# A sparse-attention and expert-router kernel: K turned a step later, rank products a step part earlier, x's first turnings around q's, and V gathered from joined rows

## The chip, the cores and the metric

The kernel runs on one core of one Trainium2 chip. The metric is device time in microseconds (us) of one launch; a profiled execution gives the trace. Engines: PE (TensorE matmul, PEld its weight loads), DVE (VectorE), ACT (ScalarE), POOL (GpSimd), SP (SyncE, whose queue issues nearly all DMAs). L with a number is a line of the kernel before.

## The reference, cut

```python
# 4 batch items, 8 heads, 768 rows, head size 64, blocks of 32 rows
scores = scale * q @ k.T                       # per batch item and head
# kept: own block and its neighbours, first and last block of rows and of keys, 3 sampled blocks per row block
attn = softmax(where(mask, scores, -1e9)) @ v
x = attn.transpose(0, 2, 1, 3).reshape(3072, 512)
# router: 8 experts, cosine similarity, argmax, softmax weight of the chosen one
for e in range(8):
    rows = expert_idx == e
    out[rows] = gate[rows, None] * (maximum(x[rows] @ w1[e], 0) @ w2[e])   # w1 512x1024, w2 1024x512
```

## The kernel before, in words

**Work units.** Attention works in 24 chunks of 128 query rows of one batch item. Two chunks of the same rows from two batch items form a pair (`pair_chunk`, 12 pairs; pairs 0 to 5 are batch items 0 and 1, pairs 6 to 11 items 2 and 3). `attention_fast` runs one loop of steps s; step s scores chunk `TURNS[s]` (order 0, 2, 1, 3, 4, 5, ...), weighs the chunk scored a step before, and turns x of the one before that. So pair p is scored in steps 2p and 2p+1 and weighed in 2p+1 and 2p+2 (p of 2 and more).

**A step on PE, in the program's order** (every engine runs its own queue in this order): `score_near` (tile `ac`, L580, L583), `score_far` (`dps`, L605, needs `kg`, gathered K columns), `turn_x` (`xg_ps`, L740), `turn_q` of the next chunk (the bank `yp`, L544; DVE evicts it in two copies, L549), `turn_k` for the K groups of table `turning` (`kps`, L526 for the first half, L532 for the second), `planned(0)`, `weigh_far` (`av<-vg,pd`, L660: the first use of a pair's gathered V), the rest of the weighing, `normalize` on DVE, `planned(1)`. In the steps that follow a chunk with the first and last blocks, `score_ends` (`bps`) comes in too.

**What sets the order.** `planned` runs entries (step, part, function) that `after_step` writes for the routing of a pair: among them `rank` (L891, L893), two small products into the same bank `yp` that turned q uses, once for each of the first three groups of six chunks; its three DVE operations read that bank. `fill_slots` (L980) uses the bank too. POOL writes `seen` (L864), which `rank` reads.

**V.** `vt[m]` holds six tiles of V of the present two batch items, 128 rows x 2 x 8 x 65 floats (64 values and a column of ones); `load_v` fills them by table `values_at` for the second half. `gather_v` brings, for each block of a pair and each of its 3 samples, 32 rows of V from DRAM into `vg_ring`, two buffers: twelve DMAs a pair (six where the pair has the first and last blocks), each of 32 x 16 runs of 64 floats. SP issues them in `fetch_all` (L497 for other loads between them, L499 for the gathers), six in step 2p-2 and the rest in step 2p-1, each behind the release of the buffer that pair p-2 used. Pair 2's twelve are all issued in step 3. `x_dram<-x` (L881) is on SP as well and waits for DVE.

The experts' stage follows from about 250 us: 23 tiles of 128 rows, two large products each.

```python
def gather_v(k, s, i=None):
    a, c = pair_chunk(s)
    t, src = k.vg_ring[s % 2], of_seq(k.v, a, i)
    for r in range(NRAND):
        for g, shift in zip(blocks_of(c), shifts(k, mybir.EngineType.SP, r, c)):
            yield in_pair(t[lanes_of(r, g), g], i)[:, :, 0:D], src[bass.ds(shift, BLK)]
```

Of the kernel before, what the change touches and what calls it, by code (L numbers as in the profile page):

```python
# [12 lines left out]
F32 = mybir.dt.float32  # L13
# [8 lines left out]
B, H, S, D = 4, 8, 768, 64  # L22
BLK = 32
NB = S // BLK
NRAND = 3
NC = S // P
# [24 lines left out]
VW = H * (D + 1)  # L51
NI = NB - 2
NCH = B * NC
DUO = 2
NS = NCH // DUO
TURNS = [0, 2, 1, 3, *range(4, NCH)]
DEN_LOW, DEN_HIGH = 0.1, 1e10
NEG = -1.0e9
LGAT = 80
# [323 lines left out]
def lanes_of(slot, g):  # L383

    if slot < 2:
        return slice(BLK + slot, NRAND * BLK, 2)
    return slice(0, BLK) if (slot + g) % 2 == 0 else slice(NRAND * BLK, P)
# [35 lines left out]
def in_pair(t, i=None):  # L423

    return t.rearrange("p i h e -> p (i h) e") if i is None else t[:, i]
# [58 lines left out]
def gather_v(k, s, i=None):  # L484

    a, c = pair_chunk(s)
    t, src = k.vg_ring[s % 2], of_seq(k.v, a, i)
    for r in range(NRAND):
        for g, shift in zip(blocks_of(c), shifts(k, mybir.EngineType.SP, r, c)):
            yield in_pair(t[lanes_of(r, g), g], i)[:, :, 0:D], src[bass.ds(shift, BLK)]  # L490


def fetch_all(k, gathers, loads):

    for i, (to, src) in enumerate(gathers):
        if i % 2 == 0 and loads:
            k.nc.sync.dma_start(out=loads[0][0], in_=loads[0][1])  # L497
            loads = loads[1:]
        k.nc.sync.dma_start(out=to, in_=src)  # L499
    for to, src in loads:  # L500
        k.nc.sync.dma_start(out=to, in_=src)
# [37 lines left out]
def turn_q(k, n):  # L539

    raw = in_pair(k.raw["q", n // DUO], n % DUO)
    ps = bank(k, "q_ps").rearrange("p (j t) -> p j t", t=P)
    for j in range(NPAIR):
        k.nc.tensor.transpose(ps[:, j], raw[:, 2 * j:2 * j + 2, :].rearrange("p h d -> p (h d)"), k.ident)  # L544
    k.qt[n] = t = k.qt_ring[k.queries % 2]
    k.queries += 1
    for h in range(2):
        rows = slice(D * h, D * (h + 1))
        k.nc.vector.tensor_copy(out=t[rows, :, h], in_=ps[rows])  # L549
# [185 lines left out]
def turn_x(k, n):  # L735

    s, i = divmod(n, DUO)
    ps = ring(k, "xg_ps", 0, 1, k.eps, [P, ND, P])
    for j in range(ND):
        k.nc.tensor.transpose(ps[:, j], k.x[s][:, i, j, 0:P], k.ident)  # L740
    if i == 0:
        k.xt[s] = k.xt_pool.tile([P, ND, DUO, P], F32, name="xt", tag="xt", bufs=1)
    k.nc.vector.tensor_copy(out=k.xt[s][:, :, i], in_=ps)  # L743
# [543 lines left out]
def after_step(n, b):  # L1287

    s = TURNS.index(DUO * b + 1) + 2
    steps = route(n, b)  # L1290
    routing = partial(next, steps, None)
    plan = [(s, 1, routing), (s + 1, 1, routing), (s + 2, 0, routing), (s + 2, 0, routing), (s + 2, 1, routing)]
    if s + 3 < NCH:
        plan += [(s + 3, 0, routing)]
    else:
        n.unwritten.append(steps)
    if b % (NC // DUO) == NC // DUO - 1 and b < NS - 1:
        plan += [(s + 3, 0, partial(rank, n, b // (NC // DUO)))]
    if DUO * (b + 1) == EARLY * NC:
        n.dispatching = partial(next, dispatch_early(n), None)  # L1300
        plan += [(s + 3 + (i + 1) // 3, int((i + 1) % 3 > 0), n.dispatching) for i in range(18)]
        plan += [(s + 9, 0, partial(fetch_rows, n, 0))]
        n.first_weights = fetch_weights(n, 0, 0, 4)
        plan += [(s + 7 + i, 1, partial(next, n.first_weights)) for i in range(4)]
        plan += [(s + 10, 1, partial(prepare, n, 0))]
    return [(min(when, NCH), part if when <= NCH else 1, what) for when, part, what in plan]


def attention_fast(n, ctx):
# [64 lines left out]
    nc.gpsimd.memset(zero, 0.0)  # L1374
    nc.sync.dma_start(n.x_dram[N:N + 1, :], zero)

    turning = {0: (4, 5), 1: (6, 7), 10: (8, 9), 11: (10, 11, 12), 12: (13, 14, 15)}
    keys_at = {2: (8, 9), 3: (10,), 4: (11,), 5: (12,), 6: (13,), 10: (14, 15)}
    values_at = {7: (0,), 8: (1,), 9: (2,), 11: (3,), 13: (4,), 15: (5,)}
    routed = {TURNS.index(DUO * b + 1) + 2: b for b in range(NS - 1)}  # L1380
    plan = []
    for s in range(NCH + 1):
        now, after, last, past = (TURNS[i] if 0 <= i < NCH else None for i in (s, s + 1, s - 1, s - 2))
        if s in routed:
            plan = after_step(n, routed[s]) + [p for p in plan if p[0] >= s]
# [6 lines left out]
        def keys_gathered():  # L1392
            if after is not None:
                gather_k(n, after)

        ends = last is not None and place(last)[1] == 0
        late_keys = s in turning and s > 0
        if now is not None:
            score_near(n, now)
            score_far(n, now)  # L1400
# [5 lines left out]
        if past is not None and past >= 2 * DUO:  # L1406
            turn_x(n, past)
        elif past is not None and past % DUO:
            turn_x(n, past - 1)
            turn_x(n, past)  # L1410
        if ends:
            score_ends(n, last, 0)
            score_ends(n, last, 2)
        elif after is not None:
            turn_q(n, after)
        for g in turning.get(s, ()):
            turn_k(n, g)
        if late_keys:
            keys_gathered()
        planned(0)  # L1420
        if s == 0:
            stack_ends(n, 1, (0, 1), 0)
# [23 lines left out]
        if ends:  # L1446
            weigh_ends(n, last, (0, 2))
            score_ends(n, last, 1)
            score_ends(n, last, 3)
            if after is not None:  # L1450
                turn_q(n, after)
        ahead, odd = s // DUO + 1, s % DUO
        loads, gathers = [], ()
        if s in (2, 3):
# [18 lines left out]
        for m in values_at.get(s, ()):  # L1473
            loads += load_v(n, 1, m)
        fetch_all(n, gathers, loads)
        if ends:
            weigh_ends(n, last, (1, 3))
        if last is not None:
# [173 lines left out]
@with_exitstack  # L1652
def kernel(
    ctx: ExitStack,
    tc: tile.TileContext,
    q: bass.AP,
    k: bass.AP,
    v: bass.AP,
    sampled_blocks: bass.AP,
    moe_expert_emb: bass.AP,  # L1660
    moe_tau: bass.AP,
    moe_w1: bass.AP,
    moe_w2: bass.AP,
    out: bass.AP,
):
    assert tuple(q.shape) == (B, H, S, D) and tuple(out.shape) == (N, DM)
    assert tuple(moe_w1.shape) == (E, DM, F) and tuple(sampled_blocks.shape) == (NB, NRAND)
    n = Net()
    n.tc, n.nc = tc, tc.nc
    n.q, n.k, n.v, n.blocks, n.out = q, k, v, sampled_blocks, out  # L1670
    n.emb, n.tau, n.w1, n.w2 = moe_expert_emb, moe_tau, moe_w1, moe_w2
    n.loaded, n.vs, n.es, n.ets, n.sums, n.x, n.rows, n.weights = {}, {}, {}, {}, {}, {}, {}, {}

    n.raw, n.nsq, n.lg, n.turned_rows, n.relu = {}, {}, {}, {}, None
    n.kt, n.qt, n.kg, n.pac, n.pd, n.pb, n.av, n.xt = ({} for _ in range(8))
    n.exact = n.attending = False
    n.const = ctx.enter_context(tc.tile_pool(name="const", bufs=1))
    n.x_dram = tc.dram_tile([N + 1, XW], F32, name="x_dram")
    n.dens = n.const.tile([P, NCH, H], F32, name="dens")

    fast(n)
    todo = n.nc.values_load(n.todo[0:1, 0:1], min_val=0, max_val=2)
    with tc.If(todo > 0):
        more(n)
# [32 lines left out]
```

## Time and profile before

| what | value |
| --- | --- |
| median of 3 runs | 625.15 us (624.96 to 627.76) |
| the profiled execution | 619.32 us, span 617.6 us |
| mean granted TensorE clock | 0.992 of full |
| busy | PE 583.4, DVE 244.6, POOL 244.6, ACT 146.4 us |
| DMA | 170.6 MB in 177,073 packets, 135,432 of them under 512 B |
| steps' starts | 0: 14.7, 1: 28.4, 2: 45.6, 3: 50.2, 4: 64.7, 5: 73.3, 7: 89.7, 9: 105.9, 13: 144.3, 15: 161.0, 17: 179.0, 22: 218.4 us |

The page says how long each engine was busy and cuts the span into 40 slices of 15.4 us. The view of waits lists what each engine stood still for, the timeline shows the instructions of an engine in order with the idle time ahead of them in brackets, and the view of windows gives busy time, granted clock and DMA load of chosen stretches. A step's start is the first `ac` product of its chunk.

### The profile page before, as it was taken

How to read it: one execution, taken by the hardware profiler on the slowest of the kernel's cores; microseconds unless marked ns; L12 is line 12 of the kernel's file. 1: busy time of each engine (PE TensorE's matmuls, PEld its weight loads, DVE VectorE, ACT ScalarE, POOL GpSimd, SP SyncE). 2: the span in 40 equal slices, each digit the busy share in tenths (PEclk: the TensorE clock that was granted, in tenths of full speed). 3: DMA queues.
4: the chain of work that ended last, by engine and by line, in shares of the span. 5: the costliest groups of instructions: out<-in, count | busy, mean ns of one | idle time of the engine just before them, and what ended most of it. 6: DMA issues, size and time to landing. Idle time of an engine off the chain costs nothing.

```text
span 617.6 us, 18763 instructions
## 1 busy us (share of the span) xinstructions
PE 583.4 (94%) x7732; PEld 451.8 (73%) x7732; DVE 244.6 (40%) x743; ACT 146.4 (24%) x287; POOL 244.6 (40%) x474
## 2 busy tenths in 40 slices
PE   7699999998989988999999999999999999999995
PEld 5588888887888977777766777755777636777772
DVE  4424667577879962457211121112122121121110
ACT  2346555565645544100000000000000000000000
POOL 2728347446766330320333334443333333334432
PEclk9799999999999999999999999999999999999999
DMA  9998798999999851899999999998999998999611
GB/s 201 235 171 192 150 169 179 187 198 210 199 196 203 180 193 39 266 402 393 406 400 392 408 396 324 340 327 307 404 408 390 398 381 309 395 400 408 226 36 35
DMA packets 177073, 170.60 MB, mean 276 GB/s; under 512 B 135432, under 2 KB 137608, under 8 KB 174162
## 3 DMA queue, kind: packets, MB, share of 16 engines
q1 hardware_dynamic: 170706, 155.61, 81.2%
q0 software_dynamic: 5216, 13.43, 6.0%
q8 instruction: 63, 1.03, 0.7%
q10 hardware_dynamic: 1056, 0.26, 0.2%
q14 instruction: 32, 0.26, 0.1%
HBM read 156.65 MB, written 12.90 MB: 275 GB/s over the span
## 4 chain that ended last, share of the span: by engine, by line
PE 75%; DVE 9%; DMA 5%; SPq 4%; ACT 2%; issue 2%; POOL 1%; POOLq 0%; DVEq 0%; ACTq 0%
PE hp L1218 26%; PE yp L1231 25%; PE av L660 7%; PE dps L605 4%; SPq L499 3%; PE hp L1263 2%; PE yp L1283 2%; DVE qt L549 2%; PE ac L580 2%; DMA vg<-in_v_dram 2%; DMA w<-in_moe_w_dram 2%; PE ac L583 2%; PE kps L526 1%; PE xg_ps L740 1%; DVE xt L743 1%
## 5 line engine op out<-in xcount | busy, mean ns | idle before, releaser
L1218 PEld LDWEIGHTS hp<-xgt,w 128*128 128x128 f32 x1472 | 167.8, 192 | 10.9 <-issue 10.2
L1218 PE MATMUL hp<-xgt,w 128*128 128x128 f32 x1472 | 169.2, 275 | 0.3 <-DMA w<-in_moe_w_dram 0.3
L1231 PE MATMUL yp<-w,h 128*128 128x512 f32 x368 | 162.0, 592 | 0.0
L1231 PEld LDWEIGHTS yp<-w,h 128*128 128x128 f32 x368 | 68.1, 190 | 76.6 <-issue 76.3
L1142 POOL DMA_INDIRECT xg<-x_dram,quarter x88 | 89.2, 1014 | 32.3 <-issue 27.4
L1244 POOL DMA_INDIRECT out_dram<-y,slot_l x20 | 20.5, 1023 | 156.0 <-DVE y L1243 156.0
L1221 ACT ACTIVATE h<-hp 128x512 f32<-128x512 f32 x23 | 13.7, 597 | 283.1 <-PE hp L1218 280.2
L1225 DVE TENSOR_SCALAR h<-hp 128x512 f32<-128x512 f32 x23 | 15.9, 691 | 126.8 <-PE hp L1218 126.8
L562 POOL COPY kg<-kt 128x128 f32 x176 | 43.8, 299 | 33.5 <-ACT kt L528 23.1
L1243 DVE TENSOR_SCALAR y<-yp,gate 128x512 f32<-128x512 f32 x20 | 15.0, 751 | 102.2 <-PE yp L1231 90.1
L511 POOL COPY vg<-vt 32x1040 f32<-32x1040 f32 (+1 forms) x45 | 43.1, 958 | 21.4 <-PE av L660 14.5
L605 PEld LDWEIGHTS dps<-qt,kg 128*64 128x64 f32 x1408 | 46.7, 138 | 0.0
L605 PE MATMUL dps<-qt,kg 128*64 128x64 f32 x1408 | 45.8, 222 | 0.0
L583 PE MATMUL ac<-qt,kt 128*64 128x256 f32 (+1 forms) x192 | 42.4, 364 | 1.2 <-ACT kt L536 1.2
L580 PE MATMUL ac<-qt,kt 128*64 128x128 f32 x352 | 42.8, 273 | 0.3 <-DVE qt L549 0.3
L580 PEld LDWEIGHTS ac<-qt,kt 128*64 128x64 f32 x352 | 37.9, 137 | 0.6 <-issue 0.5
L549 DVE COPY qt<-yp 64x512 f32<-64x512 f32 x48 | 32.8, 683 | 12.1 <-PE yp L544 11.7
L610 ACT ACTIVATE pd<-dps,bias 128x256 f32<-128x256 f32 x88 | 34.7, 476 | 8.5 <-PE dps L605 8.3
L660 PE MATMUL av<-vg,pd 128*32 128x65 f32 x1408 | 27.5, 221 | 4.1 <-DMA vg<-in_v_dram 2.0
L660 PEld LDWEIGHTS av<-vg,pd 128*32 128x32 f32 x1408 | 22.3, 109 | 8.8 <-issue 4.4
L660 PEld LDWEIGHTS av<-st,pac 128*64 128x64 f32 x704 | 22.8, 137 | 5.8 <-issue 4.8
L730 ACT ACTIVATE pac<-x 128x512 f32<-128x512 f32 x24 | 15.1, 631 | 49.5 <-DVE x L725 49.5
(244 smaller groups left out, 629.4 us busy)
## 6 DMA issues: line engine op xcount, KB each, us to landing
w<-in_moe_w_dram SPq DMA_DIRECT2D x52, 2048.0 KB, 15.2
vg<-in_v_dram SPq DMA_DIRECT2D x132, 128.0 KB, 4.4
kraw<-in_k_dram SPq DMA_DIRECT2D x32, 192.0 KB, 4.6
x_dram<-x SPq DMA_DIRECT2D x10, 516.0 KB, 5.2
qraw<-in_q_dram SPq DMA_DIRECT2D x9, 512.0 KB, 6.2
w<-in_moe_w_dram SPq DMA_DIRECT2D x8, 512.0 KB, 5.1
vt<-in_v_dram SPq DMA_DIRECT2D x10, 256.0 KB, 5.7
vt<-in_v_dram SPq DMA_DIRECT2D x5, 512.0 KB, 6.6
```

The source lines that it names most:

```text
L511: k.nc.gpsimd.tensor_copy(out=k.vg_ring[s % 2][lanes_of(NRAND, g), g, which(i)], in_=k.vt[m][rows, which(i)])
L549: k.nc.vector.tensor_copy(out=t[rows, :, h], in_=ps[rows])
L562: copy(out=t[:, :, g, lanes_of(s, g)], in_=kt[:, :, bass.ds(shift, BLK)])
L580: nc.tensor.matmul(out[0:D, j, half], lhsT=kt[:, j, at:at + D], rhs=qt[:, j, :, D * half:D * (half + 1)], start=True, stop=True)
L583: nc.tensor.matmul(out[D:P, j, half:2].rearrange("p f h t -> p h f t"), lhsT=kt[:, j, S:S + D], rhs=qt[:, j, :, D * half:P].rearrange("p h ...
L605: nc.tensor.matmul(out[D * r:D * (r + 1), NG * j + g], lhsT=kg[:, j, g, D * r:D * (r + 1)], rhs=qt[:, j, :, cols], start=True, stop=True)
L610: nc.scalar.activation(e[:, :, g].rearrange("p j h t -> p j (h t)"), out.rearrange("p (j g) h t -> p j g (h t)", g=NG)[:, :, g], ACT.Exp, ...
L660: k.nc.tensor.matmul(av[lanes, h // NPAIR, h % NPAIR * P:h % NPAIR * P + D + 1], lhsT=lhsT, rhs=rhs, start=first[0], stop=last, skip_group ...
L1142: k.nc.gpsimd.indirect_dma_start(out=x[:, g], out_offset=None, in_=quarters, in_offset=bass.IndirectOffsetOnAxis(ap=k.quarter[:, g, t:t + ...
L1218: nc.tensor.matmul(hp[:, f, :], lhsT=w1[:, d, (f0 + f) * P:(f0 + f + 1) * P], rhs=xt[:, d, :], start=(d == 0), stop=(d == ND - 1))
L1231: nc.tensor.matmul(yp, lhsT=h[:, f, :], rhs=w2[:, f, :], start=(f == 0), stop=(f == NF - 1))
L1244: k.scattered = nc.gpsimd.indirect_dma_start(out=k.out[:, :], out_offset=bass.IndirectOffsetOnAxis(ap=slot, axis=0), in_=y[:, :], in_offse ...
```

## The change

Four things, by tables and by the order of calls:

- **K's turning**: groups 4 to 7 (batch item 1) were turned two in step 0 and two in step 1; now all four in step 1, and in the steps with end blocks behind the last `score_ends` and `turn_q` (`turn_keys`).
- **x's first turnings**: in steps 4 and 5 two chunks of x are turned; the second now comes behind `turn_q`.
- **Rank products**: from `planned(0)` of step s + 3 to `planned(1)` of step s + 2, so to the end of the step before.
- **V in joined rows**: `join_v` writes the six tiles `vt` to a DRAM tensor `joined[a]` of 768 rows x 1040 floats (4160 bytes), for the first half behind the gathers of step 3, for the second in steps 12 (three tiles) and 13 (three). The gathers of pairs 3, 4, 5, 8, 9, 10 and 11 read whole rows of it, 32 per DMA. V's tiles of the second half are loaded sooner: two in step 8, one in each of steps 9, 10 and 11.

```diff
--- before.py
+++ after.py
@@ -54,6 +54,7 @@
 DUO = 2
 NS = NCH // DUO
 TURNS = [0, 2, 1, 3, *range(4, NCH)]
+JOINED = (3, 4, 5, 8, 9, 10, 11)
 DEN_LOW, DEN_HIGH = 0.1, 1e10
 NEG = -1.0e9
 LGAT = 80
@@ -487,7 +488,16 @@
     t, src = k.vg_ring[s % 2], of_seq(k.v, a, i)
     for r in range(NRAND):
         for g, shift in zip(blocks_of(c), shifts(k, mybir.EngineType.SP, r, c)):
-            yield in_pair(t[lanes_of(r, g), g], i)[:, :, 0:D], src[bass.ds(shift, BLK)]
+            if s in JOINED:
+                yield t[lanes_of(r, g), g].rearrange("p i h e -> p (i h e)"), k.joined[a][bass.ds(shift, BLK)]
+            else:
+                yield in_pair(t[lanes_of(r, g), g], i)[:, :, 0:D], src[bass.ds(shift, BLK)]
+
+
+def join_v(k, a, m):
+
+    rows_of = k.vt[m].rearrange("p i h e -> p (i h e)")
+    return [(k.joined[a][lo:lo + rows.stop - rows.start], rows_of[rows]) for rows, lo in pieces(m)]
 
 
 def fetch_all(k, gathers, loads):
@@ -1295,7 +1305,7 @@
     else:
         n.unwritten.append(steps)
     if b % (NC // DUO) == NC // DUO - 1 and b < NS - 1:
-        plan += [(s + 3, 0, partial(rank, n, b // (NC // DUO)))]
+        plan += [(s + 2, 1, partial(rank, n, b // (NC // DUO)))]
     if DUO * (b + 1) == EARLY * NC:
         n.dispatching = partial(next, dispatch_early(n), None)
         plan += [(s + 3 + (i + 1) // 3, int((i + 1) % 3 > 0), n.dispatching) for i in range(18)]
@@ -1374,9 +1384,10 @@
     nc.gpsimd.memset(zero, 0.0)
     nc.sync.dma_start(n.x_dram[N:N + 1, :], zero)
 
-    turning = {0: (4, 5), 1: (6, 7), 10: (8, 9), 11: (10, 11, 12), 12: (13, 14, 15)}
+    turning = {1: (4, 5, 6, 7), 10: (8, 9), 11: (10, 11, 12), 12: (13, 14, 15)}
     keys_at = {2: (8, 9), 3: (10,), 4: (11,), 5: (12,), 6: (13,), 10: (14, 15)}
-    values_at = {7: (0,), 8: (1,), 9: (2,), 11: (3,), 13: (4,), 15: (5,)}
+    values_at = {7: (0,), 8: (1, 2), 9: (3,), 10: (4,), 11: (5,)}
+    joined_at = {3: (0, range(NC)), 12: (1, range(3)), 13: (1, range(3, NC))}
     routed = {TURNS.index(DUO * b + 1) + 2: b for b in range(NS - 1)}
     plan = []
     for s in range(NCH + 1):
@@ -1394,7 +1405,14 @@
                 gather_k(n, after)
 
         ends = last is not None and place(last)[1] == 0
-        late_keys = s in turning and s > 0
+        late_keys = s in turning
+
+        def turn_keys():
+            for g in turning.get(s, ()):
+                turn_k(n, g)
+            if late_keys:
+                keys_gathered()
+
         if now is not None:
             score_near(n, now)
             score_far(n, now)
@@ -1407,16 +1425,15 @@
             turn_x(n, past)
         elif past is not None and past % DUO:
             turn_x(n, past - 1)
-            turn_x(n, past)
         if ends:
             score_ends(n, last, 0)
             score_ends(n, last, 2)
         elif after is not None:
             turn_q(n, after)
-        for g in turning.get(s, ()):
-            turn_k(n, g)
-        if late_keys:
-            keys_gathered()
+        if past is not None and past < 2 * DUO and past % DUO:
+            turn_x(n, past)
+        if not ends:
+            turn_keys()
         planned(0)
         if s == 0:
             stack_ends(n, 1, (0, 1), 0)
@@ -1449,6 +1466,7 @@
             score_ends(n, last, 3)
             if after is not None:
                 turn_q(n, after)
+            turn_keys()
         ahead, odd = s // DUO + 1, s % DUO
         loads, gathers = [], ()
         if s in (2, 3):
@@ -1473,6 +1491,9 @@
         for m in values_at.get(s, ()):
             loads += load_v(n, 1, m)
         fetch_all(n, gathers, loads)
+        if s in joined_at:
+            a, some = joined_at[s]
+            fetch_all(n, (), [piece for m in some for piece in join_v(n, a, m)])
         if ends:
             weigh_ends(n, last, (1, 3))
         if last is not None:
@@ -1676,6 +1697,7 @@
     n.exact = n.attending = False
     n.const = ctx.enter_context(tc.tile_pool(name="const", bufs=1))
     n.x_dram = tc.dram_tile([N + 1, XW], F32, name="x_dram")
+    n.joined = [tc.dram_tile([S, DUO * VW], F32, name=f"joined{a}") for a in range(B // DUO)]
     n.dens = n.const.tile([P, NCH, H], F32, name="dens")
 
     fast(n)
```

**PE, the end of step 0 and the start of step 1.** `kps` is K being turned, `ac` and `dps` are scores. Before:

```order
L605 MATMUL dps<-qt_117,kg 64x64 x16
L544 MATMUL yp_245<-ident,qraw 128x128 x4
L526 MATMUL kps<-ident,kraw 64x128 x24
L580 MATMUL ac<-qt_118,kt_103 64x128
L583 MATMUL ac<-qt_118,kt_103 64x2x2x64
```

And of the change, the same place and then the later one in step 1:

```order
L615 MATMUL dps<-qt_119,kg 64x64 x16
L554 MATMUL yp_247<-ident,qraw 128x128 x4
L590 MATMUL ac<-qt_120,kt_105 64x128
L593 MATMUL ac<-qt_120,kt_105 64x2x2x64
L590 MATMUL ac<-qt_120,kt_105 64x128 x2
...
L637 MATMUL bps<-qt_119,kt_105 64x128 x2
L637 MATMUL bps<-qt_119,kt_105 128x128 x5
L646 MATMUL bps<-qt_119,kt_105 64x64 x24
L554 MATMUL yp_247<-ident,qraw 128x128 x4
L536 MATMUL kps<-ident,kraw 64x128 x48
L670 MATMUL av<-vt_106,pb_113 64x65
```

Step 1's scores now follow q's turning at once; K's four groups (x48) stand between the second turning of q and the second half of the ends' weighing.

**SP, the end of step 3 and the start of step 4.** Before, the last gathers of pair 2 (`vg_113`) and the first of pair 3 (`vg_114`):

```order
L499 DMA vg_113<-in_v_dram 32x16x64
L499 ISA
L499 DMA vg_113<-in_v_dram 32x16x64
L395 TENSOR_LOAD offset
L497 DMA kraw<-in_k_dram 128x6x64
L499 ISA
L499 DMA vg_114<-in_v_dram 32x16x64
```

Of the change:

```order
L509 DMA vg_115<-in_v_dram 32x16x64
L511 DMA joined_61<-vt_106 32x1040
L511 DMA joined_61<-vt_106 96x1040
L511 DMA joined_61<-vt_107 128x1040
L511 DMA joined_61<-vt_108 128x1040
L511 DMA joined_61<-vt_109 128x1040
L511 DMA joined_61<-vt_110 128x1040
L511 DMA joined_61<-vt_111 128x1040
L396 TENSOR_LOAD offset
L507 DMA kraw<-in_k_dram 128x6x64
L509 ISA
L509 DMA vg_116<-joined_61 32x1040
```

Seven writes come in between, and the first gather of pair 3 reads what they write.

**PE, the rank products of the third group.** Before, in step 22 behind q's turning, while the slot products (`lanes`, 12 of them) end step 21:

```order
L772 MATMUL av<-sel,part 128x8 x2
L740 MATMUL xg_ps_1330<-ident,x 128x128 x4
L544 MATMUL yp_245<-ident,qraw 128x128 x4
L891 LDWEIGHTS ones_b
L891 MATMUL yp_245<-seen,ones_b 128x56
L893 LDWEIGHTS before
L893 MATMUL yp_245<-oh,before 128x48
L660 MATMUL av<-vg_113,pd 32x65 x32
```

Of the change, at the end of step 21, ahead of the slot products:

```order
L670 MATMUL av<-st_117,pac 64x65 x16
L901 LDWEIGHTS ones_b
L901 MATMUL yp_247<-seen,ones_b 128x56
L903 LDWEIGHTS before
L903 MATMUL yp_247<-oh,before 128x48
L990 LDWEIGHTS lanes
L990 MATMUL yp_247<-val,lanes 128x10
```

Rank and slot products use the same bank `yp`, now one right behind the other.

## Rows read from the trace of the kernel before

**Rows 1.** The page, busy time of each engine and DMA slices (15.4 us each).

```profile
PE 583.4 (94%) x7732; PEld 451.8 (73%) x7732; DVE 244.6 (40%) x743; ACT 146.4 (24%) x287; POOL 244.6 (40%) x474
...
DMA  9998798999999851899999999998999998999611
```

**Rows 2.** Waits of PE over the span: us in total, times, longest us.

```profile
PE kps L526 <- DMA kraw<-in_k_dram: 5.2, 1, 5.2
PE yp L891 <- DVE qt L549: 4.0, 3, 1.9
PE av L660 <- DMA vg<-in_v_dram: 2.0, 3, 1.1
...
PE xg_ps L740 <- DVE xt L743: 1.6, 2, 0.9
```

**Rows 3.** Timeline of PE, steps 0 to 2: start us, us, instruction [idle before].

```profile
18.23 0.66 PE L544 MATMUL yp<-ident,qraw 128*128 128x128 f32 x4
24.11 4.61 PE L526 MATMUL kps<-ident,kraw 128*64 128x128 f32 x47 [5.23 <-DMA kraw<-in_k_dram]
...
34.94 2.84 PE L526 MATMUL kps<-ident,kraw 128*64 128x128 f32 x48
...
45.60 0.32 PE L580 MATMUL ac<-qt,kt 128*64 128x128 f32 x1
```

**Rows 4.** Timeline of DVE, step 0: the eviction of turned q.

```profile
18.96 1.39 DVE L549 COPY qt<-yp 64x512 f32<-64x512 f32 x2
```

**Rows 5.** Windows: stretch, length, PE busy (count), granted clock, DMA share, GB/s.

```profile
24.00:26.00 2.00, 1.89 (x16) 0.50 1.20 311
...
28.00:30.00 2.00, 2.00 (x35) 1.00 1.39 194
...
124.00:164.00 40.00, 37.37 (x896) 1.00 1.02 201
300.00:400.00 100.00, 100.00 (x580) 1.00 1.00 380
```

**Rows 6.** Timeline of PE, the three rank products and the slot products (L980).

```profile
121.67 0.20 PE L891 MATMUL yp<-seen,ones_b 128*128 128x56 bf16 x1 [0.40 <-DVE qt L549]
...
176.85 0.20 PE L891 MATMUL yp<-seen,ones_b 128*128 128x56 bf16 x1 [1.71 <-DVE qt L549]
...
217.80 0.68 PE L980 MATMUL yp<-val,lanes 128*128 128x10 bf16 x12
...
223.84 0.20 PE L891 MATMUL yp<-seen,ones_b 128*128 128x56 bf16 x1 [1.93 <-DVE qt L549]
```

**Rows 7.** Timelines of POOL and DVE at the end of step 21.

```profile
217.81 0.72 POOL L864 TENSOR_TENSOR seen<-seen,oh 128x8 bf16<-128x8 bf16 x2 [8.73 <-DVE oh L860]
...
219.58 0.20 DVE L872 RECIPROCAL x<-gate 128x8 f32<-128x8 f32 x1 [0.22 <-POOL gate L869]
```

**Rows 8.** Timeline of SP: the last of pair 2's gathers, pair 3's first and last.

```profile
62.04 6.49 SPq L499 DMA_DIRECT2D vg<-in_v_dram  x8
...
72.00 1.46 SPq L499 DMA_DIRECT2D vg<-in_v_dram  x2
...
85.22 1.92 SPq L499 DMA_DIRECT2D vg<-in_v_dram  x2
```

**Rows 9.** The gathers' line: issue in ns (min/median/max), landing in us.

```profile
L499 SPq DMA_DIRECT2D vg<-in_v_dram x132: 325/597/3652, 12.5 to 214.4; - x132
...
DMA to landing us min/median/max: 2.9/4.4/7.3
```

**Rows 10.** Timeline of PE: first weighing of pairs 3, 6 and 8.

```profile
94.40 1.11 PE L660 MATMUL av<-vg,pd 128*32 128x65 f32 x64
...
150.38 0.73 PE L660 MATMUL av<-vg,pd 128*32 128x65 f32 x4 [0.29 <-DMA vg<-in_v_dram]
...
183.76 1.15 PE L660 MATMUL av<-vg,pd 128*32 128x65 f32 x64
```

**Rows 11.** Waits of SP over the span, the line that writes x.

```profile
SPq L881 <- DVE l L851: 3.1, 4, 1.5
```

## The prediction

> **What bounds the kernel now.** I read the page first. TensorE is busy 94% of the span, and the 16 DMA engines are nearly as full while attention runs (the first 230 us) [rows 1]. So the rest of the trace is asked two things: where does TensorE stand still, and which of these stops would a lighter DMA load or another order remove. The list of TensorE's waits answers the first: 5.2 us for K's raw rows, 4.0 us in three stops of the rank products, 2.0 us for gathered V, 1.6 us for an eviction of turned x [rows 2]. The change touches all four, and nothing in the expert stage, so at most some 13 us of 617.6 are at stake, plus what a stop does to the clock. Then come the sync queue (SP), which issues every gather in order, and the moments at which TensorE first multiplies a gathered pair.
>
> **K's turning.** Before, TensorE ends its q turning at 18.23 + 0.66 = 18.9 us, idles 5.23 us for K, and then turns 47 tiles in 4.61 us; 48 more of the same kind take 2.84 us later [rows 3]. The clock was granted at 0.50 (1.2 GHz) in 24 to 26 us and at 1.00 (2.4 GHz) from 28 us [rows 5]: the idle time halved it, and that cost 4.61 - 2.78 = 1.83 us more. After, all four K groups are turned at the end of step 1, when K has long landed, and step 1's first scores only wait for the eviction of q, 18.96 + 1.39 = 20.35 us [rows 4], so 1.46 us of idling stays. Gain: 5.23 + 1.83 - 1.46 = **5.6 us**. V's gathers and tiles for step 1 are loads of before that are now wanted some 10 us sooner; I allow nothing for them, and 1 us in the range.
>
> **x's first turnings.** In steps 4 and 5 the second turning of x waits for the eviction of the first, 1.6 us in two stops [rows 2]. With q's turning between them that bank is free in time: **1.6 us**, at least 1 us, since VectorE also has q's two evictions to do.
>
> **Rank products.** They stand right behind q's turning and share its bank: stops of 0.40, 1.71 and 1.93 us [rows 6]. At the end of the step before, the bank is free. The first two are then gained (2.1 us): their counts are ready in time. The third is not. In step 21 GpSimd makes the counts at 217.81 + 0.72 = 218.53 us, and the bank is given on to the 12 slot products behind, which today start at 217.80 us [rows 6, 7]. VectorE reads the ranks only behind its reciprocal, which ends at 219.78 us [rows 7], with three small operations, about 0.6 us. So TensorE stands there some 2.6 us in place of 1.93: **loss 0.7 us**.
>
> **V in long rows.** A gather of 512 packets of 256 bytes becomes 32 rows of 4160. The nearest rows for the price are the DMA rates: 201 GB/s at share 1.02, so 197 GB/s, where packets are small, 380 GB/s in the expert stage with its long rows [rows 5]. That is 131,072 B / 197 = 0.67 us against 133,120 B / 380 = 0.35 us: 0.32 us saved, 78 times, 25 us of the engines' time. Added are twice 768 rows, 3.19 MB / 380 = 8.4 us each time (at 197 it would be 16 us).
>
> What decides is when they run. The first seven writes stand behind pair 2's gathers, which SP ends issuing at 62.04 + 6.49 = 68.5 us. Today pair 3's first gather goes out at 72.00 us [rows 8]; now its source is what was just written, so SP holds it, and all behind it (K, q, V, x to DRAM), until all seven have landed. The engines first finish the gathers ahead, about 4.4 us each from issue [rows 9], so the writes' data start near 72 and end near **80.4 us: 8.4 us late**. Pair 3's last gather today starts near 86.3 us [rows 8] and lands 4.4 later [rows 9], 90.7; with 12 gathers at 0.32 less it lands at 90.7 + 8.4 - 3.8 = 95.3 us. TensorE first wants it at 94.40 us [rows 10], and after the gains above at 94.4 - 7.2 = 87.2. It waits **8.1 us**: the start's gain is given back, and 0.9 us beyond it. Such a stop also halves the clock again, 1.8 us by the case above. At step 8 the new kernel is 2.7 us behind.
>
> From there TensorE follows the queue or its own work, whichever is later. Step 9's wait for V (1.1 us of the 2.0, [rows 2]) goes: +1.6. The first rank: +1.2. For the queue, pairs 3 to 5 save 36 x 0.32 = 11.5 us; V's tiles for the second half come sooner, two more (524,288 B / 197 = 2.7 us each) ahead of pair 6, one more ahead of pair 7; and of SP's 3.1 us of waits for VectorE [rows 11] I let 1.5 be absorbed by its lateness. Pair 6: 8.4 - 11.5 + 5.4 - 1.5 = +0.8, no new stop, and what TensorE waited for that pair (0.29 us, [rows 10]) goes: +0.9. Pair 7 has three tiles' writes (4.2 us) ahead of half of it: 8.4 - 11.5 + 2.7 + 4.2 - 1.5 = +2.3, and TensorE waits until then: +2.3. The second rank: +0.6. Pair 8 waits for the landing of the rest of the writes (1.5 us, half the least landing time of rows 9): 8.4 - 11.5 + 8.4 + 1.5 - 1.5 - 3.8 = +1.5; it has no slack today: its last V rows land about when TensorE starts on it at 183.76 us [rows 10]. So +1.5. Pairs 9 to 11 are light. The third rank: **+2.2 us** in all.
>
> The profiled execution took 619.3 us, the median of the runs is 625.15, 5.8 us more. I add the 2.2 us to both: 621.5 in its own time, **627.3 us** in the median. A measurement of this kernel tells about 0.5%, 3.1 us, from no change; this is inside.
>
> **Rivals.** *The writes cost little* (faster): if their data overlap the gathers ahead, or a joined gather costs clearly less than 0.35 us with its neighbours, pair 3 lands by 91 us. The stop is then 3.5 us, pairs 6 to 8 are in time, and the sum is 5.6 + 1.6 + 2.1 - 0.7 + 2.0 (V's waits) - 3.5 = 7.1 us: 618.0 us. For it: DMA shares of 0.8 to 0.9 before 124 us are not 1. Against it: SP's wait is for a landing, which no share shortens.
>
> *A gather's price is by transfer and not by packet* (slower). Issue takes 325 ns at least and 597 in the median, and landing 2.9 us at least, whatever is moved [rows 9]; if that is what a gather costs, the relief goes while the writes stay. With half the relief pair 8 is 1.5 + 48 x 0.16 = 9.2 us late, with the third rank 9.9: 635.0 us; with none 642.7. It turns slower than the measurement's limit once a joined gather saves under 0.30 us. For it: SP issues eight gathers in 6.49 us, 0.81 each [rows 8], slower than the 0.67 the engines need, so issue may be the limit. Against it: a gather's landing takes 2.9 to 7.3 us [rows 9], so the load counts.
> The Trainium skill ("DMA: Bandwidth & Descriptors", section "Bandwidth") speaks for this rival: it ties the rate to a transfer's size, 138 GB/s at 64 KB and 341 at 1 MB, and a gather of 133 KB keeps its size. By that a joined gather would cost about 0.8 us (an estimate from that page), and the sum would be near 642. No run here shows long rows in so small a transfer; the 256-byte rows' 0.67 us lies near it.
>
> *Rows do not stay whole*: written or read in pieces the packets would stay small; this ends as the last rival. 3 in 100.
>
> **How the numbers follow.** Forecast and its near neighbours (inside 3.1 us) 0.40; faster 0.24, of which the full rival is half; slower 0.36, because the chain from pair 3 to pair 8 adds up several small latenesses and every one of them can be larger. The forecast's own range is 623 to 631 (write rate, 0.32 us by a quarter, 1 us at the start). The 8-in-10 range reaches into both rivals: 619 to 633.
>
> **What would show it.** No K wait near 19 us, full clock until step 7, and step 2 at 40 instead of 45.6 us. SP: seven writes near 69 us, then a hole until about 80. TensorE: a stop of 6 to 9 us in front of the seventh step's weighing (87 to 95 us) and a granted clock of 0.5 behind it; V waits at steps 13 to 17 of 1 to 3 us; the third rank with a wait for GpSimd. DMA packets under 512 B fall from 135,000 to about 95,000. I am wrong if that hole is under 5 us, if the stop in step 7 is under 4, or if pairs 6 to 8 are waited for longer than 5 us in all.

## The result: 632.5 us, 1.2% slower, and the profile after

The changed kernel takes 632.5 us in the median of 20 runs (627.0 to 639.2); the kernel before, run beside it, 624.85 (20 runs). The ratio is **1.0123, 95% interval 1.0102 to 1.0144**: 7.7 us slower. The prediction was 627.3, range 619 to 633. The profiled execution of the change took 636.77 us (span 635.0), 4 us over its median, and the one before 619.32, 5.5 us under its own, so stops are read here for their place and kind, and sizes are taken from the experiments.

The page of the changed kernel, busy time, DMA slices and packets:

```profile
PE 591.4 (93%) x7732; PEld 458.1 (72%) x7732; DVE 238.6 (38%) x743; ACT 146.3 (23%) x287; POOL 244.9 (39%) x474
...
DMA  8989879999868860399999999998999998999611
...
DMA packets 141393, 177.15 MB, mean 279 GB/s; under 512 B 95720, under 2 KB 97896, under 8 KB 138482
```

Short packets fell from 135,432 to 95,720, as they should, and the DMA slices are lighter than in [rows 1], yet TensorE is no better used. Its waits over the span (us in total, times, longest):

```profile
PE yp L554 <- DMA qraw<-in_q_dram: 5.4, 3, 2.3
...
PE av L670 <- DMA vg<-joined: 3.4, 6, 1.1
PE av L670 <- DMA vg<-in_v_dram: 3.4, 4, 2.3
...
PE yp L901 <- POOL seen L874: 1.3, 2, 0.7
```

Against [rows 2]: the 5.2 us for K are gone, and of the 4.0 us of the rank products 1.3 us of waiting for GpSimd are left. In their place stand 6.8 us (before 2.0) for gathered V and waits for q's raw rows. Of their 5.4 us, 2.3 are the first load in the setup, where the kernel before waits 1.7; new are 1.2 us near 34 us and 1.9 in step 7. Where the steps start, us, read as the first `ac` product of each; "order alone" and "second half" are experiments below:

| step | before | change | order alone | order and second half |
| --- | --- | --- | --- | --- |
| 2 | 45.60 | 42.58 | 41.40 | 45.14 |
| 7 | 89.67 | 88.19 | 85.87 | 90.25 |
| 8 | 97.61 | 104.19 | 93.81 | 98.20 |
| 13 | 144.26 | 150.09 | 140.63 | 146.39 |
| 14 | 153.74 | 164.32 | 149.79 | 159.85 |
| 23 | 226.02 | 240.17 | 222.50 | 234.56 |

Two steps carry most of the loss. Step 7 takes 16.00 us (before 7.94) and step 13 takes 14.23 (before 9.48). SP around the first writes, in its timeline (start, us, instruction):

```profile
69.93 7.46 SPq L511 DMA_DIRECT2D joined<-vt  x7
78.51 0.40 SPq L507 DMA_DIRECT2D kraw<-in_k_dram  x1
83.68 1.19 SPq L509 DMA_DIRECT2D vg<-joined  x2
```

Pair 3's first gather goes out at 83.68 us, 72.00 before [rows 8]. What SP waited for there, over 70 to 90 us (us, times, longest), and then ahead of pair 8, over 170 to 190 us:

```profile
SPq L509 <- DMA joined<-vt: 4.4, 2, 3.0
...
SPq L509 <- DMA joined<-vt: 4.3, 1, 4.3
```

The stop on TensorE in step 7, in its timeline [idle before]:

```profile
94.69 0.66 PE L554 MATMUL yp<-ident,qraw 128*128 128x128 f32 x4 [1.93 <-DMA qraw<-in_q_dram]
97.08 0.40 PE L670 MATMUL av<-vg,pd 128*32 128x65 f32 x2 [1.73 <-issue]
97.98 0.43 PE L670 MATMUL av<-vg,pd 128*32 128x65 f32 x2 [0.51 <-DMA vg<-joined]
99.22 0.42 PE L670 MATMUL av<-vg,pd 128*32 128x65 f32 x2 [0.81 <-DMA vg<-joined]
100.08 1.83 PE L670 MATMUL av<-vg,pd 128*32 128x65 f32 x57 [0.43 <-DMA vg<-joined]
```

These are 5.41 us of idling; the rest of the 8.06 us is work at half clock. Windows of the changed kernel (stretch and length, busy time and count of PE, PEld, DVE, ACT and POOL, granted clock, DMA share, GB/s):

```profile
74.00:80.00 6.00, 5.27 (x141) 4.22 (x138) 2.96 (x6) 4.26 (x8) 4.88 (x12) 1.00 1.02 399
82.00:84.00 2.00, 1.65 (x52) 1.51 (x48) 1.79 (x12) 1.67 (x3) 0.00 (x0) 1.00 0.11 25
...
98.00:102.00 4.00, 2.76 (x66) 2.26 (x70) 0.00 (x0) 0.00 (x0) 3.64 (x8) 0.50 1.05 223
...
160.00:164.00 4.00, 4.00 (x93) 3.19 (x89) 0.00 (x0) 0.37 (x1) 3.88 (x4) 0.50 0.87 194
...
183.50:188.00 4.50, 4.50 (x127) 4.27 (x126) 3.19 (x14) 2.41 (x6) 4.12 (x11) 1.00 0.43 122
...
195.80:201.10 5.30, 4.76 (x126) 3.93 (x127) 2.51 (x13) 1.98 (x4) 3.52 (x9) 1.00 0.88 250
```

The writes move at 399 GB/s and fill the engines for 6 us and more; behind them the engines stand almost empty (share 0.11) while SP waits for the landing. The clock, the last but two of the columns, is at 0.50 (1.2 GHz) behind the stop of step 7 and again in step 13, where TensorE waited for pair 6:

```profile
158.23 0.32 PE L670 MATMUL av<-vg,pd 128*32 128x65 f32 x2 [2.34 <-DMA vg<-in_v_dram]
```

The last two windows are joined gathers, from the first of pair 8 on. SP issues them one behind the other (its timeline below). In the first window the engines are less than half busy, but SP had issued nothing from 178.90 to 183.51 us, so their share is still rising there. In the later one, with the gathers as close, the share is 0.88.

```profile
177.34 1.56 SPq L891 DMA_DIRECT2D x_dram<-x  x1
183.51 4.96 SPq L509 DMA_DIRECT2D vg<-joined  x6
...
195.83 4.45 SPq L509 DMA_DIRECT2D vg<-joined  x6
```

Six take 4.96 or 4.45 us, 0.83 or 0.74 each. For pair 8 TensorE waits 1.7 us in step 17, the longest stop of which is

```profile
195.78 0.27 PE L670 MATMUL av<-vg,pd 128*32 128x65 f32 x2 [1.14 <-DMA vg<-joined]
```

### The profile page after: what moved, and what is told of

It is laid out like the page before. It is cut to its first block, busy times and chain, and to the rows that moved or that the text cites. A ratio compares the mean times of both kernels' runs of the same rounds, so it can differ in the third digit from the quotient of the medians.

```text
span 635.0 us, 18785 instructions
## 1 busy us (share of the span) xinstructions
PE 591.4 (93%) x7732; PEld 458.1 (72%) x7732; DVE 238.6 (38%) x743; ACT 146.3 (23%) x287; POOL 244.9 (39%) x474
## 2 busy tenths in 40 slices
DMA packets 141393, 177.15 MB, mean 279 GB/s; under 512 B 95720, under 2 KB 97896, under 8 KB 138482
## 4 chain that ended last, share of the span: by engine, by line
PE 70%; SPq 8%; DVE 8%; DMA 6%; issue 3%; ACT 2%; POOL 1%; another core or an unknown queue 1%; DVEq 0%; POOLq 0%; ACTq 0%
PE hp L1228 25%; PE yp L1241 24%; SPq L509 6%; PE av L670 4%; PE dps L615 3%; PE hp L1273 2%; PE yp L1293 2%; DVE qt L559 2%; PE ac L590 2%; DMA vg<-in_v_dram 2%; DMA w<-in_moe_w_dram 2%; PE ac L593 2%; DVE xt L753 1%; DMA kraw<-in_k_dram 1%; PE kps L536 1%
## 5 line engine op out<-in xcount | busy, mean ns | idle before, releaser
L590 PE MATMUL ac<-qt,kt 128*64 128x128 f32 x352 | 44.2, 278 | 4.6 <-DVE qt L559 2.6
L615 PE MATMUL dps<-qt,kg 128*64 128x64 f32 x1408 | 47.3, 224 | 1.1 <-issue 1.1
L593 PE MATMUL ac<-qt,kt 128*64 128x256 f32 (+1 forms) x192 | 43.7, 371 | 1.2 <-ACT kt L546 1.2
L670 PE MATMUL av<-vg,pd 128*32 128x65 f32 x1408 | 30.4, 229 | 8.8 <-DMA vg<-joined 3.4
L620 ACT ACTIVATE pd<-dps,bias 128x256 f32<-128x256 f32 x88 | 34.7, 476 | 10.9 <-PE dps L615 10.8
L670 PEld LDWEIGHTS av<-vg,pd 128*32 128x32 f32 x1408 | 24.3, 114 | 14.7 <-issue 8.6
L670 PE MATMUL av<-st,pac 128*64 128x65 f32 x704 | 27.4, 231 | 0.2 <-issue 0.2
```

The source lines that it names most:

```text
L590: nc.tensor.matmul(out[0:D, j, half], lhsT=kt[:, j, at:at + D], rhs=qt[:, j, :, D * half:D * (half + 1)], start=True, stop=True)
L593: nc.tensor.matmul(out[D:P, j, half:2].rearrange("p f h t -> p h f t"), lhsT=kt[:, j, S:S + D], rhs=qt[:, j, :, D * half:P].rearrange("p h ...
L615: nc.tensor.matmul(out[D * r:D * (r + 1), NG * j + g], lhsT=kg[:, j, g, D * r:D * (r + 1)], rhs=qt[:, j, :, cols], start=True, stop=True)
L620: nc.scalar.activation(e[:, :, g].rearrange("p j h t -> p j (h t)"), out.rearrange("p (j g) h t -> p j g (h t)", g=NG)[:, :, g], ACT.Exp, ...
L670: k.nc.tensor.matmul(av[lanes, h // NPAIR, h % NPAIR * P:h % NPAIR * P + D + 1], lhsT=lhsT, rhs=rhs, start=first[0], stop=last, skip_group ...
```

## Experiments

Ratios are to the kernel before, run on the same chip, with 95% intervals; 0.1% is 0.6 us.

### The order alone

`JOINED` and `joined_at` empty, `values_at` as before; the three changes of order stay.

```diff
-    values_at = {7: (0,), 8: (1, 2), 9: (3,), 10: (4,), 11: (5,)}
-    joined_at = {3: (0, range(NC)), 12: (1, range(3)), 13: (1, range(3, NC))}
+    values_at = {7: (0,), 8: (1,), 9: (2,), 11: (3,), 13: (4,), 15: (5,)}
+    joined_at = {}
```

> Order part alone (K's turning, x, rank products); no joined rows, V's tiles loaded as before. Theory A (the order gains, the rows cost): step 2 starts about 3 us sooner than before (not the 5.6 of the prediction, because loads of step 1 are now waited for), and the time is about 4 us under the kernel before: 620 to 622. Rival B (the start's gain is swallowed at the next wait for gathered V, since the DMA queue sets the pace): 624 to 625.5, no change. Rival C (the order itself costs): over 627.

Measured: 620.42 us, **0.9961** (0.9931 to 0.9991), about 2.4 us gained. Theory A. Step 2 starts 4.2 us sooner, and from there to step 23 the lead stays near 3.5 to 4 us (table, last column but one). The order gains, though far less than the 8.6 us of the prediction's four terms. One of these terms can be read here: x's turnings kept most of their 1.6 us in steps 4 and 5, half of it now in front of the products behind them.

```profile
65.86 0.66 PE L750 MATMUL xg_ps<-ident,x 128*128 128x128 f32 x4 [0.35 <-DVE xt L753]
67.88 0.64 PE L772 MATMUL xg_ps<-xt,en 128*32 128x256 f32 x8 [0.32 <-DVE xt L753]
75.09 0.66 PE L750 MATMUL xg_ps<-ident,x 128*128 128x128 f32 x4 [0.42 <-DVE xt L753]
77.11 0.64 PE L772 MATMUL xg_ps<-xt,en 128*32 128x256 f32 x8 [0.32 <-DVE xt L753]
```

### The rows alone

The order of before; joined rows and V's sooner tiles as in the change.

```diff
-    turning = {1: (4, 5, 6, 7), 10: ...
+    turning = {0: (4, 5), 1: (6, 7), 10: ...
-        plan += [(s + 2, 1, partial(rank, ...
+        plan += [(s + 3, 0, partial(rank, ...
```

> Joined rows and V's sooner tiles alone, in the order of before. Theory A: TensorE comes 3 us later to step 7 and waits 5 us there in place of 8, so most of the order's gain is not missed: 632 to 635, 1 to 3 us above the whole change. If the two parts simply add (order -4, rows +11.5) it is 636 or more. Rival C: 628 to 630, under the whole change.

Measured: 631.89 us, **1.0143** (1.0102 to 1.0185), 8.9 us slower, just under what theory A gave (632 to 635) and above rival C (628 to 630); the whole change is 1.0123. The rows, with V's sooner tiles, are the cause. With the order's -2.4 the parts sum to +6.5 against +7.7 measured, inside the intervals; that TensorE's lead is swallowed at step 7 can't be told from a plain sum.

### Pair 3 without joined rows

```diff
-JOINED = (3, 4, 5, 8, 9, 10, 11)
+JOINED = (4, 5, 8, 9, 10, 11)
```

> The whole change, but pair 3 gathers from V itself, so that nothing waits for the landing of the first seven writes; the writes still stand ahead of it. Theory A1 (the hold behind the landing is what costs, as the prediction had it): the stop at step 7 falls from about 7.9 to under 4 us and the time to 627 or less. Rival A2 (the writes' own 3.19 MB ahead of pair 3 cost, the hold only some 3 us, and its twelve gathers lose 0.24 us each of relief): the stop stays between 5 and 9 us, the time 630 to 634.

Measured: 631.75 us, **1.0134** (1.0095 to 1.0172), as the whole change. Rival A2. Nothing waits for the writes to land, and step 7 takes 15.96 us, as long as in the change (16.00). Its stops, in TensorE's timeline:

```profile
94.80 0.80 PE L670 MATMUL av<-vg,pd 128*32 128x65 f32 x4 [3.72 <-issue]
97.25 0.42 PE L670 MATMUL av<-vg,pd 128*32 128x65 f32 x2 [1.65 <-DMA vg<-joined]
97.90 1.83 PE L670 MATMUL av<-vg,pd 128*32 128x65 f32 x57 [0.22 <-DMA vg<-in_v_dram]
```

(Releasers are inferred: pair 3 reads no joined row here, whatever name stands in the second row.) So SP's wait for the landing is not what the stop rests on: the writes' data ahead of pair 3 are enough, and what the hold takes, pair 3's lighter gathers give back.

### The second half alone

`JOINED = (8, 9, 10, 11)`, no writes in step 3; all else as in the change.

> The whole change without the first seven writes: pairs 3 to 5 gather from V itself, pairs 8 to 11 from joined rows, V's tiles of the second half sooner. Theory A2: no stop at step 7, step 8 starts about 4 us before the old start (93 to 94 us); from step 13 on, two V tiles (5.4 us) ahead of pair 6 and the writes ahead of pair 8 cost 4 to 7 us: 623 to 628. If the first half is the whole cause: 620 to 621.

Measured: 628.01 us, **1.0071** (1.0042 to 1.0100), 6.9 us over the order alone, at the upper edge of what theory A2 gave (623 to 628). No stop at step 7 (it takes 7.95 us), but step 13 takes 13.45. The second half costs more than the first (below). Its profiled execution shows something else as well: its start was lost.

```profile
34.02 1.08 PE L554 MATMUL yp<-ident,qraw 128*128 128x128 f32 x4 [2.88 <-DMA qraw<-in_q_dram]
...
45.14 0.32 PE L590 MATMUL ac<-qt,kt 128*64 128x128 f32 x1
```

The window that follows that stop:

```profile
34.00:38.00 4.00, 3.98 (x32) 3.67 (x34) 1.47 (x3) 0.00 (x0) 0.00 (x0) 0.50 0.87 186
```

In the order alone the same stop is 1.16 us, the clock stays at 1.00 and step 2 starts at 41.40. K's turning, now behind this stop, runs at half clock where the stop is long: 3.7 us between two executions of kernels whose work is the same up to there.

### V's sooner tiles alone

The order, no joined rows, `values_at` as in the change.

> Order part, and V's tiles of the second half loaded sooner; no joined rows. Theory D (two V tiles, 5.4 us of data, now stand ahead of pair 6 and make TensorE late at step 13 and the granted clock halve there, which nothing gives back): step 13 takes 12 to 14 us in place of 9.2, time 623 to 625, some 3 to 4 us over the order alone (620.4). Rival (the queue has room for them, and the writes and the hold cost all): 620 to 621.

Measured: 624.08 us, **0.9997** (0.9965 to 1.0029), 2.2 us over the order alone, with intervals that overlap. Theory D in place, and a little low in price: step 13 takes 13.69 us, with this stop in front of pair 6:

```profile
152.09 0.67 PE L670 MATMUL av<-vg,pd 128*32 128x65 f32 x4 [2.47 <-DMA vg<-in_v_dram]
```

### The second half written and not read

As in the last experiment, V's sooner tiles included, and `joined_at = {12: ..., 13: ...}` with `JOINED = ()`: the rows are written, V itself is gathered.

> As the kernel with sooner V tiles, and the second half's tiles are also written in rows in steps 12 and 13, but no gather reads them (V itself is gathered): nothing waits for their landing. Theory D2 (the writes' bytes cost: three tiles ahead of half of pair 7, three ahead of pair 8): 3 to 5 us over the kernel with sooner tiles, 627 to 629, like the second half with its gathers (628.0). Rival (the hold until the landing costs, which is 4.3 us of SP's time ahead of pair 8 in the whole change): not over 1 us above the kernel with sooner tiles, and 3 us or more under 628.

Measured: 627.0 us, **1.0063** (1.0035 to 1.0091). The writes cost 4.1 us more than the sooner tiles alone; reading them, with its hold and its lighter gathers, changes +0.08% (the second half alone, 1.0071), nothing that can be told. D2: the writes' bytes cost. What the hold costs, if anything, the lighter gathers gave back.

### The first half alone

`JOINED = (3, 4, 5)`, `joined_at = {3: ...}`, `values_at` as before.

> Order part, joined rows for pairs 3 to 5 alone, V's tiles of the second half at their old steps. Theory A2: the stop at step 7 is there in full (step 7 takes 15 to 16 us), and the 36 lighter gathers then give back some of the lateness of the queue but not of TensorE: 625 to 628. If the costs of the halves add up to the whole (620.4 + 7.6 for the second half, 630.6 for both): 623.

Measured: 623.22 us, **0.9989** (0.9958 to 1.0020), 1.7 us over the order alone, with intervals that overlap; step 7 takes 17.15 us. A miss: I had 625 to 628. The stop is there in full, but the lighter gathers return most of it (the first half written and not read, below), and the halves add within the intervals: -2.4, +1.7 and +6.9 make +6.2, measured +7.7 (6.4 to 9.0).

### The third rank left in place

The order alone, and the third `rank` at `(s + 3, 0)` as before.

```diff
-        plan += [(s + 2, 1, partial(rank, n, b // (NC // DUO)))]
+        plan += [(s + 2, 1, ...) if b < 8 else (s + 3, 0, ...)]
```

> Order part alone, but the third rank products stay where they were before (behind q's turning of step 22). Theory E (at the end of step 21 they wait for GpSimd and hold the slot products, so that move loses 1 to 2 us): 618.5 to 619.5, 1 to 2 us under the order part (620.4). Rival (its wait lies beside other waits and moves nothing): 620 to 621.

Measured: 619.63 us, **0.9949** (0.9916 to 0.9981). It is 0.8 us under the order alone, where the prediction had 0.7, but the intervals overlap: unclear. In the change the third rank waits 0.72 us for GpSimd and the slot products 1.19 for VectorE behind it, together as much as the one stop of 1.93 before [rows 6], so these waits show no loss:

```profile
231.38 0.19 PE L901 MATMUL yp<-seen,ones_b 128*128 128x56 bf16 x1 [0.72 <-POOL seen L874]
...
232.78 0.45 PE L990 MATMUL yp<-val,lanes 128*128 128x10 bf16 x12 [1.19 <-DVE mine L907]
```

### K's turning alone

> K's turning alone a step later; x's turnings and all rank products as before. Theory F (the stop for K at 18.9 us becomes a stop for q's raw rows at the end of step 1, 1.2 us in some executions and near 3 us, with the granted clock at 0.50 behind it, in others): no stop for K, a stop of 1 to 3 us in front of the turning of q near 33 us, time 621 to 623.5, 0 to 2 us under the kernel before (623). If the prediction's 5.6 us were right: 617.5.

Measured: 621.01 us, **0.9972** (0.9950 to 0.9995): 1.7 us gained (0.3 to 3.1), not 5.6. Theory F: no stop for K, and a stop of 2.67 us for q's raw rows at 33.4 us.

### The first half written and not read

The order, `joined_at = {3: ...}`, `JOINED = ()`.

> Order part, the first half's tiles written in rows in step 3, but no gather reads them; V's tiles of the second half at their old steps. Theory G (bytes against bytes: seven writes make the queue 8 to 9 us late, and 36 lighter gathers take some 0.2 us each off that): the stop at step 7 is there all the same (7 us or more), and without lighter gathers the queue stays late, so pairs 4 to 6 are waited for too: 626 to 630, 3 us or more over the first half with its gathers (623.2). Rival (the hold costs as much as the lighter gathers save): 622.5 to 624.

Measured: 626.39 us, **1.0065** (1.0037 to 1.0094). Theory G: step 7 takes 16.77 us without any hold, and without lighter gathers the time is 0.76% (4.7 us) over the first half with them. That is the relief, less what the hold takes back: 4.7 / 36 = **0.13 us a gather**, by the intervals some 0.06 to 0.20. The writes alone cost 1.04% of 623, 6.5 us (1.0065 against 0.9961).

### q ahead of K in the setup

The order with the third rank kept; V's last tiles and the raw q of step 2 are loaded ahead of K's groups 4 and 5.

```diff
-    for g in range(NPAIR, 6):
-        fetch_all(n, (), load_k(n, g))
-    fetch_all(n, (), values[3:])
+    fetch_all(n, (), values[3:] + load_q(n, 0, 1))
+    for g in range(NPAIR, 6):
+        fetch_all(n, (), load_k(n, g))
...
-    fetch_all(n, gather_v(n, 1), load_q(n, 0, 1) + load_q(n, 1, 1))
+    fetch_all(n, gather_v(n, 1), load_q(n, 1, 1))
```

> Order part with the third rank products kept in their old place, and in the setup the raw q of step 2's chunk and V's last tiles are loaded ahead of K's groups 4 to 7, which nothing needs until the end of step 1. Theory F: the stop for q near 33 us goes (1.2 to 3 us), and with it the halved clock of some executions: step 2 starts at 40 to 41 us, time 617 to 618.5, 1 to 2.5 us under the same kernel with the old order of loads (619.6). Rival (the stop moves on to K's turning or to gathered V, since the queue's load is the same): 619 to 620.5.

Measured: 620.06 us, **0.9944** (0.9923 to 0.9965), the same as without (0.9949). The rival. Step 2 starts at 40.10 us, the time that the prediction gave, and the lead is gone in the step itself:

```profile
40.10 0.32 PE L590 MATMUL ac<-qt,kt 128*64 128x128 f32 x1
...
45.12 1.94 PE L670 MATMUL av<-vg,pd 128*32 128x65 f32 x58 [0.49 <-DMA vg<-in_v_dram]
48.58 0.27 PE L590 MATMUL ac<-qt,kt 128*64 128x128 f32 x1
```

Four short waits for pair 1's gathers, then half clock (0.62 over 44 to 48 us), and step 3 starts at 48.58; in the kernel of the experiment with the third rank kept it starts at 46.20.

### Gathers from two queues

The order with the third rank kept; from pair 3 on the third sample's gathers are issued by ScalarE.

```diff
-        for g, shift in zip(blocks_of(c), shifts(k, mybir.EngineType.SP, r, c)):
+        other = r == NRAND - 1 and s >= 3
+        queue = mybir.EngineType.Activation if other else mybir.EngineType.SP
+        for g, shift in zip(blocks_of(c), shifts(k, queue, r, c)):
+            if other:
+                k.nc.scalar.dma_start(...)
```

> Order part with the third rank products kept, V gathered as before (64-float runs), but from pair 3 on the gathers of the third sample (four of a pair's twelve) are issued from ScalarE's queue. Theory H (SP's own pace, about 0.85 us from gather to gather against 0.72 for a joined one, and not the 16 engines' bytes, is what a gather costs while attention runs): SP gets through a pair a third sooner, the waits for gathered V from step 7 on (about 3 us with their kind in the kernel without this) shrink to under 1 us, time 616 to 618.5. Rival (the engines' packets are the limit): 619 to 620.5. If ScalarE's exponentials are held behind its gathers: over 621.

Measured: 627.57 us, **1.0082** (1.0047 to 1.0116), and it doesn't decide. V is no longer among TensorE's larger waits, as theory H wanted, but SP now waits for the other queue's gathers to land, and so writes x late: VectorE waits for that write, and TensorE for VectorE, 8.7 us in step 8. The time lies where the third case had it (over 621), but ScalarE is held by x there, not by its own gathers. SP's waits from 60 to 240 us, VectorE in step 8, and TensorE's waits:

```profile
SPq L513 <- DMA vg<-in_v_dram: 37.3, 13, 7.4
```

```profile
105.74 0.69 DVE L739 TENSOR_TENSOR x<-av,inv 128x512 f32<-128x512 f32 x1 [10.67 <-DMA x_dram<-x]
```

```profile
PE av L786 <- DVE x L886: 8.7, 1, 8.7
```

Whether SP's pace is the limit can't be read from a kernel in which SP waits 37 us for something new.

## Why the prediction was right in its direction and short in its size

What was right: the stop in front of step 7's weighing with the clock at 0.50 behind it (the step is 8.06 us longer, 5.4 of it idling, where 8.1 of waiting and 1.8 of clock were forecast), and that it swallows the start's gain; the packets under 512 B (95,720, forecast about 95,000); the third rank's wait for GpSimd; pair 8's wait (1.7 us in the profiled execution, forecast 1.5). Step 13's V wait of 2.5 us fits the list of signs, but not the working, which had no new stop for pair 6.

The time, 632.5, is 5.2 us over the forecast and outside its own range, 623 to 631. It lies within 619 to 633 by 0.5 us, since that range reached towards the slower rival. At step 8 the change is 6.6 us behind (forecast 2.7), at step 23 14.2, both between the two profiled executions.

Where the miss lies can be said from the runs. The order was to gain 8.6 us and gained 2.4: 6.2 us, about all of the difference between +7.7 and the forecast +2.2. Joined rows and sooner tiles cost 10.1 us over the order alone (1.0123 against 0.9961), where the forecast implies 2.2 + 8.6 = 10.8. That these agree is luck: the forecast put most of it on the first half, which cost 1.7 us, and the second half cost 6.9. Four steps failed:

**"V's gathers and tiles for step 1 are loads of before that are now wanted some 10 us sooner; I allow nothing for them."** This is where 5.6 us became 1.7. The term counted what TensorE no longer waits for, and not what it now reaches too early: first q's raw rows (1.2 to 2.9 us, at times with half clock), and with these out of the way pair 1's gathers (the experiment with q ahead of K). In both experiments (K's turning alone, q ahead of K) TensorE met the next late load instead: a later wait takes what an earlier one gave.

**"0.32 us saved" per joined gather.** It was taken from the 16 engines' rates, for the long rows from the expert stage. Three things show less. The relief measured, the hold's cost taken off, is 0.13 us in the first half (read against not read) and nothing that can be told in the second. The issue on SP got shorter by as much (ns, min/median/max):

```profile
L509 SPq DMA_DIRECT2D vg<-joined x78: 315/467/4326, 83.7 to 226.0; - x78
...
L509 SPq DMA_DIRECT2D vg<-in_v_dram x54: 335/597/3994, 12.7 to 174.8; - x54
```

597 - 467 = 130 ns, and the same 42 gathers of pairs 8 to 11 tell it too, in the order alone and in the change:

```profile
L509 SPq DMA_DIRECT2D vg<-in_v_dram x42: 325/602/3182, 161.4 to 209.3; - x42
...
L509 SPq DMA_DIRECT2D vg<-joined x42: 315/467/1669, 183.5 to 226.0; - x42
```

And the engines saved less than 0.32 as well: by the traces' records of single packets, one of 256 bytes takes 20.7 ns in the mean (order alone), 32 to an engine, 0.66 us a gather; one of 4160 bytes, read, 247 ns (change), two to an engine, 0.49 us. That is 0.17 us. So SP's issue and the engines' packets both give a relief of the size measured, and which of them sets it stays open: the run that was to isolate it didn't. The second rival's half relief, 0.16 us, gave 635.0; its reason (price by transfer, not by packet) is not shown.
The Trainium skill ("DMA: Bandwidth & Descriptors", section "Bandwidth") has the rate go with the transfer's size, from which the prediction estimated 0.8 us a joined gather. SP's 0.74 to 0.83 us from one to the next lies there; no run here tells whether data or issue makes it so.

**"What decides is when they run ... SP holds it."** The hold is real, 4.4 us of SP's time ahead of pair 3, and I had said I would be wrong if it was under 5. I was: with the hold taken away (pair 3 unjoined) or with nothing read at all (first half written only) step 7 takes 15.96 and 16.77 us. The writes' data were the cost: by the trace's landings the last gather ahead of them lands at 74.0 us and the last write at 83.4, 9.4 us (forecast 8.4). Pair 3's last gather landed at 100.0 us in place of 95.3.

**The second half, "+0.8 no new stop ... +2.3 ... +1.5".** It cost 6.9 us over the order alone: 2.2 for V's sooner tiles and 4.1 for the writes, with nothing back from reading. Pair 6 had no room for two tiles: 2.5 us of waiting and half clock in step 13, and a stop as long with V's sooner tiles alone, with neither writes nor joined rows. The relief that was to pay for them, 36 x 0.32 = 11.5 us, was 4.7. The hold ahead of pair 8 was 4.3 us (forecast 1.5).

The x turnings and first two ranks were 3.7 us in the sum. In the order alone the two ranks' stops are gone (2.1 us), but x's turnings still wait 1.4 us of the 1.6 (rows there). In time, K's turning alone (0.9972) and the order with the third rank kept (0.9949) differ by 1.4 us, inside their intervals; what the two are worth together stays open.

Nothing with joined rows beat the order alone. The best measured are the order with the third rank kept (0.9949) and the same with q ahead of K (0.9944): some 3 us under the kernel before.

## What to carry to other kernels

Price a lighter transfer twice, by its queue's issue and by the engines' time for its packets, and from rows of the stage in which it runs: the rate of another stage gave 0.32 us here, and 0.13 came. Data written to make later reads cheaper are loads like any other: count how many reads of the path they must pay for (here 3.19 MB, 6.5 us in the first half and 4.1 in the second, against 0.13 us a gather). When a wait at the head of a load-bound stage is taken away, name the next load that the engine will ask for, or the gain is not there.

## What was not expected of the hardware

SP's issue of a gather depends on how its bytes lie: 0.60 us in the median for 512 runs of 256 bytes, 0.47 us for 32 rows of 4160, nearly the same bytes.
The Trainium skill ("DMA: Bandwidth & Descriptors", section "Issuing engines are not separate DMA queues") calls the time to initiate a transfer usually small relative to the transfer. Beside the time to landing (2.9 us at least, [rows 9]) the trace agrees. Beside the engines' own time it differs: at 399 GB/s, the rate of the writes, 133,120 bytes are 0.33 us, and by their packets' records 0.49, near the 0.47 us of their issue.
A packet of 4160 bytes took 247 ns in the mean when it was read by a gather, and 186 when it was written.
And a stop of 2.88 us ahead of 34 us left the granted clock at 0.50 (34 to 38 us) where one of 1.16 us left it at 1.00, so that two executions part by 3.7 us before step 2.
